# Four output stores of a two-stage attention kernel, moved behind a crossbar transfer in SyncE's order

## The chip, the core and the metric

The kernel runs on one core of one Trainium2 chip. Its metric is the device time of one execution in microseconds. Each engine of the core has its own instruction queue, which it works off in order: PE (TensorE) multiplies, DVE (VectorE) and ACT (ScalarE) read its results out of PSUM, POOL (GpSimd) masks and issues the loads, SP (SyncE) does no arithmetic here and issues DMAs. An engine waits for another one by semaphore. The DMA engines are shared by all queues.

## What is computed

Two stages, the second on the output of the first. Batch 8, 8 heads, 576 positions, head size 64; all inputs and the output are float32.

```python
def _attn_ref(q, k, v):                       # q, k, v: (8, 8, 576, 64)
    k_p = k.reshape(B, H, Sp, pool, D).mean(axis=3)      # 576 keys pooled by 8 to 72
    v_p = v.reshape(B, H, Sp, pool, D).mean(axis=3)
    scores = scale * np.matmul(q, k_p.transpose(0, 1, 3, 2))
    ...                                        # softmax over the 72 keys
    return np.matmul(attn, v_p)

def _moe_ref(x, w_gate, wq, wk, wv, wo):      # x: (8, 576, 512), 4 experts of size 64
    logits = x @ w_gate
    ...                                        # the two largest of four, softmax weights w
    for e in range(E):
        q = x @ wq[e]; k = x @ wk[e]; v = x @ wv[e]
        ...                                    # causal softmax attention over 576 positions
        ye = a @ v @ wo[e]
        ...                                    # out += weight of expert e * ye
    return out                                 # (8, 576, 512)
```

## The kernel before

The whole program is one list of tokens, the string SEQ (lines 622 to 693). The loop behind it (line 696) takes the tokens in order and lets each one emit its instructions; every engine's queue thus gets its instructions in the order in which they stand in SEQ. A token is a name with indices, a colon, the batch, and where needed the PSUM bank behind an @; a d at the end puts a copy on DVE instead of ACT, a p at the end of a y leaves the store to a later token. Capital letters are matmuls, small letters mostly what reads their result. The work of several batches is interleaved, so that batch 0 is in its last stage while batch 4 is in its first.

For this change these tokens matter:

- **L_q, L_k, L_v** (load, line 112): the loads of one batch's q in four quarters, and of k and v in three thirds each, issued by POOL (line 125). They change float32 into bfloat16 on the way. There are three raw buffers for each of q, k and v (NRAW, line 53), so the loads of a batch wait until the batch three earlier has been read.
- **u** (turn, line 292): a DVE transpose of one half of a batch's q (line 297). It needs all four quarters of that batch. u1:5 and u0:5 are those of batch 5.
- **T and t** (lines 559 and 564): PE transposes an expert pair's result, a copy brings it out of PSUM into oT. t02:1 is a copy of 64 columns of batch 1 on DVE; it stands in SEQ between u1:5 and u0:5, and it frees PSUM bank 2, into which O20:3 writes, the next output matmuls of the first stage that PE has in its order.
- **F** (crossbar, line 574): for batches 2 to 5 the same step is done by a DMA transpose issued by SP, from osc to oT; F01 and F11 carry the 64 positions behind 512 (line 577), F00 and F10 the first 512 (line 580).
- **Y and y** (lines 582 and 592): the output projection of 128 positions and its copy into an output tile ofin of 128 x 512 float32, 256 KB. The pool of these tiles has nine buffers (line 69), taken in turn; a new tile waits for the store of the tile nine earlier.
- **zs** (line 711, z in line 607): the store of such a tile, issued by SP (line 615; line 611 for the tile shared by two batches).

SP's whole work is two loads at the start, then the stores and the crossbar transfers. SP issues in the order of SEQ, and a transfer whose input isn't ready holds back all that stand behind it. In the order of before, after the two loads: zs3:0, zs1:0, zs2:0, zs3:1, F01:2, F00:2, F11:2, F10:2, F01:3, zs0:1, zs2:1, F00:3, zs3:2, F11:3, F10:3, zs1:1 and so on.

Y4:3 reads the tails that F01 and F11 of batches 2 and 3 bring; Y3:3, Y0:3, Y1:3 and Y2:3 read what F00:3 and F10:3 bring.

Of the kernel before, what the change touches and what calls it, by code (L numbers as in the profile page):

```python
# [21 lines left out]
def kernel(  # L22
# [584 lines left out]
    def z(b, c, queue):  # L607
# [42 lines left out]
        P_t0:2@7 v0:3d P_k1:3@5 L_q1:6 e11:4 t12:0d p_t0:2d g2:2 u1:5 V1:3@4 p_k1:3 L_q2:6 T02:1@2 E2:4@06 v1:3 D0:4@3  # L650
        t02:1d u0:5 e21:4 O20:3@2 PK:5@5 e20:4 D1:4@4 d0:4 o20:3 O11:4@0 kc:5 S02:2@6 d1:4 L_q3:6 S11:2@2 T12:1@1 kt:5d
        x1:4 P_q0:3@5 t12:1d g3:2 s11:2 L_v0:6 o11:4 B00:1@1 P_k0:3@4 bz00:1 s02:2 bg00:1 a11:2 b00:1 P_t0:3@0 p_q0:3d
        x0:4 S10:2@2 L_v1:6 p_t0:3d S12:2@6 O10:4@5 s10:2 p_k0:3d PV:5@0 a02:2 o10:4 O01:4@1 O00:4@4 vc:5 L_v2:6 D2:4@2
# [14 lines left out]
        x0:6 O01:6@4 a10:4 p_t0:5d e20:6 PV:7@5 b10:3 e21:6 O11:6@6 o01:6 O00:6@0 vc:7 F11:3 D2:6@7 O10:6@1 S01:4@2
        o00:6 d2:6 g0:4 S02:4@4 V3:5@7 o11:6 s01:4 F10:3 P_q1:5@0 v3:5d s02:4 a01:4 o10:6 S11:4@2 S01:5@6 p_q1:5d s11:4
        S00:4@4 a02:4 P_k0:6@1 g5:4 g1:5 g6:4 s01:5 g7:4 a11:4 Y4:3@0 g8:4 p_k0:6d V2:6@2 s00:4 a01:5 g9:4 Y1:1@3 v2:6d  # L670
        Y3:3@1 y4:3dp y1:1p a00:4 E0:7@46 y3:3p g2:5 zs1:1 Y0:0@3 zs4:3 g3:5 e01:7 g4:5 zs3:3 u1:7 V3:6@2 V1:6@1 y0:0p
        v3:6d Y2:2@0 g0:5 v1:6d e00:7 E1:7@26 zs0:0 y2:2dp Y4:1@1 e11:7 g5:5 zs2:2 B00:4@0 g6:5 y4:1dp P_k1:6@4 e10:7
        bz00:4 zs4:1 bg00:4 B11:4@1 b00:4 p_k1:6 g7:5 E2:7@26 x2:6 O01:7@0 bz11:4 g8:5 e21:7 D1:7@4 g9:5 O11:7@5 e20:7
        bg11:4 O20:6@6 d1:7 b11:4 O10:7@7 D2:7@2 O00:7@3 o20:6 F11:4 D0:7@1 x1:7 O20:7@4 P_q1:6@6 d0:7 o11:7 x0:7
        B10:4@1 o10:7 V0:6@5 d2:7 o01:7 x2:7 Y1:3@2 p_q1:6 P_q0:6@7 o20:7 v0:6 o00:7 y1:3p S02:5@4 bz10:4 p_q0:6 zs1:3
        S03:5@2 bg10:4 B01:4@6 b10:4 s03:5 g1:6 V0:7@7 s02:5 F10:4 a03:5 bz01:4 P_t0:6@2 bg01:4 b01:4 v0:7 S12:5@0
        a02:5 p_t0:6d g0:6 S11:5@4 F01:4 S00:6@6 s12:5 g2:6 V3:7@3 g3:6 g4:6 B01:5@2 s00:6 v3:7d F00:4 a12:5 Y2:3@0
        bz01:5 V4:7@3 bg01:5 s11:5 b01:5 V2:7@1 a00:6 y2:3dp Y0:3@2 v2:7 S10:5@6 a11:5 zs2:3 v4:7 y0:3dp S12:6@4
        S01:6@0 s10:5 B00:5@3 g5:6 zs0:3 g6:6 g7:6 P_t0:7@2 s12:6 g8:6 a10:5 g9:6 P_q0:7@6 p_t0:7d s01:6 bz00:5 a12:6
        bg00:5 Y1:2@2 b00:5 V1:7@7 p_q0:7d y1:2p F00:5 a01:6 S10:6@0 v1:7 S11:6@4 zs1:2 S02:6@2 s10:6 B10:5@6 g1:7  # L680
        F01:5 g2:7 Y0:2@7 s02:6 bz10:5 a10:6 B11:5@0 bg10:5 b10:5 P_k0:7@1 s11:6 bz11:5 a02:6 bg11:5 b11:5 F10:5
        B00:6@6 y0:2dp Y3:4@2 p_k0:7 a11:6 Y1:4@0 bz00:6 y3:4p zs0:2 bg00:6 F11:5 B11:6@1 b00:6 y1:4p S02:7@4 zs3:4
        bz11:6 S01:7@2 g0:7 bg11:6 S00:7@6 zs1:4 s02:7 b11:6 P_q1:7@0 g3:7 g4:7 g5:7 s00:7 g6:7 B10:6@1 a02:7 T00:6@4
        P_k1:7@5 bz10:6 bg10:6 p_q1:7 t00:6d a00:7 b10:6 s01:7 T11:6@4 Y1:5@6 p_k1:7d Y3:5@7 t11:6d y1:5p S03:6@0 a01:7
        S10:7@2 y3:5dp S11:7@4 s03:6 zs1:5 Y2:5@6 s10:7 g7:7 a03:6 zs3:5 g8:7 T10:6@7 Y0:5@0 t10:6d y2:5p B01:6@1 g9:7
        a10:7 y0:5dp B00:7@7 s11:7 Y0:4@2 zs2:5 bz01:6 zs0:5 B02:6@0 bg01:6 b01:6 y0:4p Y2:4@6 a11:7 bz02:6 bz00:7
        Y4:5@1 bg02:6 bg00:7 zs0:4 b02:6 y2:4p S12:7@2 b00:7 y4:5p S03:7@4 B10:7@0 zs2:4 T01:6@7 s12:7 Y1:6@6 bz10:7
        zs4:5 t01:6d B12:6@1 bg10:7 b10:7 Y3:6@7 y1:6p bz12:6 a12:7 T00:7@2 bg12:6 B01:7@0 b12:6 y3:6p zs1:6 t00:7d
        T10:7@6 Y2:6@1 bz01:7 t10:7 zs3:6 bg01:7 B11:7@7 b01:7 y2:6p Y1:7@6 bz11:7 s03:7 Y0:6@0 bg11:7 zs2:6 b11:7
        y1:7p Y0:7@1 a03:7 y0:6dp T11:7@7 zs1:7 T01:7@6 B02:7@4 t11:7d t01:7 T02:6@5 T12:6@2 zs0:6 B12:7@0 y0:7p bz02:7  # L690
        Y3:7@3 bg02:7 bz12:7 t02:6 t12:6 Y2:7@6 bg12:7 zs0:7 b12:7 y3:7p b02:7 T12:7@2 y2:7p T02:7@7 t12:7d zs3:7
        t02:7d zs2:7 Y4:7@0 ya4:7 yb4:7d
# [83 lines left out]
```

## Time and profile before

| what | us |
|---|---|
| median of three runs | 155.64 (155.61 to 155.65) |
| the profiled execution's own time | 155.6 |
| its span in the profile | 153.9 |
| PE busy | 143.7 (93%) |
| ACT busy | 137.5 (89%) |
| DVE busy | 125.2 (81%) |
| POOL busy | 88.9 (58%) |

The profile is of one execution. Its span begins with the first instruction on an engine and ends with the last; the execution's own time is 1.7 us longer. Times in the profile are microseconds from the span's start unless marked ns. L615 is line 615 of the kernel; a name like out_dram<-ofin says what is written from what. SPq is SP's instruction queue, PEld TensorE's weight load. A timeline gives the start, the duration, the engine, the line, the operation and its tiles, how many instructions are merged (x2), and in brackets how long the engine was idle before and what ended that. The table of stretches gives for each stretch its length, the busy time of PE, PEld, DVE, ACT and POOL with their counts of instructions, the clock granted to TensorE, the mean busy share of the DMA engines over the stretch in us and the GB/s moved. The chain of waits is the work that ended last, followed back from the end: at each step to what released it, or to the instruction ahead on the same engine.

### The profile page before, as it was taken

The numbers are of one execution on the slowest core, as the hardware profiler recorded it, in microseconds if no ns is written. First come the engines' busy times: TensorE is split into PE (matmuls) and PEld (weight loads), VectorE is DVE, ScalarE is ACT, GpSimd is POOL, SyncE is SP. The second block draws the span as 40 slices with busy tenths as digits, with TensorE's granted clock in tenths as the row PEclk, the third lists the DMA queues.
The fourth block names the chain that finished last, engine by engine and source line by source line (L and its number), as shares of the span: only waits on it lengthen the run. The fifth ranks groups of instructions, "written<-read, shape, count | busy, mean of one in ns | idle before, by whom it ended". The sixth has DMA issues, their size and how long they took to land.

```text
span 153.9 us, 5467 instructions
## 1 busy us (share of the span) xinstructions
PE 143.7 (93%) x2131; PEld 78.9 (51%) x2131; DVE 125.2 (81%) x407; ACT 137.5 (89%) x255; POOL 88.9 (58%) x160
## 2 busy tenths in 40 slices
PE   6698998999999999989999999999999999999970
PEld 2232453455654366445745565474556666546640
DVE  1863926889899889979999999999998987987860
ACT  3469579999999999989999999999999999999970
POOL 6996488999789988854999332053300344443200
PEclk9999999999999999999999999999999999999996
DMA  4999999999999999999999991361192343368894
GB/s 123 244 186 184 178 179 179 180 179 190 179 183 180 183 177 181 213 248 182 182 178 213 181 111 38 83 205 38 68 291 59 104 103 101 92 208 301 290 380 159
DMA packets 68746, 26.67 MB, mean 173 GB/s; under 512 B 62704, under 2 KB 63728, under 8 KB 68720
## 3 DMA queue, kind: packets, MB, share of 16 engines
q0 software_dynamic: 57264, 14.72, 95.9%
q1 hardware_dynamic: 11088, 10.88, 22.4%
q10 hardware_dynamic: 368, 0.72, 1.5%
q8 instruction: 16, 0.26, 0.7%
q14 instruction: 10, 0.08, 0.2%
HBM read 30.42 MB, written 9.44 MB: 259 GB/s over the span
## 4 chain that ended last, share of the span: by engine, by line
PE 65%; DMA 9%; ACT 9%; POOL 8%; issue 3%; DVE 3%; SPq 0%; DVEq 0%; POOLq 0%
PE psum L220 62%; DMA qraw<-in_q_dram 6%; ACT eta L330 4%; DMA xT<-in_k_dram 4%; POOL qraw L125 3%; POOL kraw L125 2%; ACT etb L493 2%; PE psum L208 2%; POOL etb L510 2%; PE psum L229 1%; DVE qT L297 1%; ACT rza L353 1%; ACT rza L349 1%; POOL vraw L125 1%; DVE kf L277 1%
## 5 line engine op out<-in xcount | busy, mean ns | idle before, releaser
L493 ACT ACTIVATE etb<-psum 128x1024 bf16<-128x1024 f32 x48 | 47.3, 1031 | 0.7 <-PE psum L220 0.4
L510 POOL TENSOR_SCALAR_AFFINE_SELECT etb<-etb 128x256 bf16<-128x256 bf16 x64 | 25.7, 414 | 30.0 <-ACT etb L493 29.4
L330 ACT ACTIVATE eta<-psum 96x1024 bf16<-96x1024 f32 (+1 forms) x48 | 36.1, 811 | 0.5 <-PE psum L220 0.2
L220 PEld LDWEIGHTS <-etb 128*128 128x128 bf16 x480 | 18.6, 97 | 7.6 <-issue 2.8
L376 DVE TENSOR_TENSOR xT<-psum,rza 128x512 bf16<-128x512 f32 x32 | 20.5, 682 | 2.0 <-ACT rza L353 1.9
L125 POOL DMA_DIRECT2D qraw<-in_q_dram x29 | 19.1, 660 | 4.4 <-DMA vraw<-in_v_dram 2.7
L220 PE MATMUL psum<-vaug,etb 128*128 128x65 bf16 x480 | 21.0, 193 | 0.0
L125 POOL DMA_DIRECT2D kraw<-in_k_dram x25 | 19.0, 766 | 3.3 <-PE psum L220 1.0
L125 POOL DMA_DIRECT2D vraw<-in_v_dram x24 | 18.5, 773 | 3.6 <-PE psum L220 1.6
L220 PE MATMUL psum<-wop,oT 128*128 128x512 bf16 (+1 forms) x74 | 20.3, 373 | 0.3 <-DVE oT L211 0.3
L220 PE MATMUL psum<-wvg,xT 128*128 128x260 bf16 x144 | 20.5, 274 | 0.0
L220 PE MATMUL psum<-xT,wqp 128*128 128x64 bf16 (+1 forms) x128 | 19.6, 286 | 0.0
L220 PE MATMUL psum<-xT,wkp 128*128 128x512 bf16 (+1 forms) x128 | 19.5, 286 | 0.0
L552 DVE TENSOR_TENSOR osc<-psum,gt 128x256 bf16<-128x256 f32 (+2 forms) x40 | 16.7, 423 | 1.0
L220 PE MATMUL psum<-qk 64*128 64x64 bf16 (+4 forms) x192 | 16.1, 277 | 0.2
L220 PEld LDWEIGHTS <-xT 128*128 128x128 bf16 x144 | 12.7, 97 | 6.3 <-issue 2.5
L211 DVE CAST qk<-psum 128x512 bf16<-128x512 f32 (+1 forms) x24 | 14.6, 616 | 1.1 <-PE psum L220 0.5
L297 DVE STREAM_TRANSPOSE qT<-qraw 128x576 f32<-128x576 f32 (+1 forms) x17 | 13.2, 790 | 2.8 <-DMA qraw<-in_q_dram 2.3
L220 PE MATMUL psum<-qT,kpT 32*128 32x64 bf16 (+1 forms) x256 | 13.3, 289 | 1.5 <-ACT eta L330 0.6
L211 ACT COPY ofin<-psum 128x512 f32<-128x512 f32 (+1 forms) x25 | 14.0, 584 | 0.8 <-PE psum L220 0.5
L220 PE MATMUL psum<-eta,vp 96*32 96x512 bf16 (+1 forms) x256 | 13.1, 288 | 0.9 <-DVE oT L211 0.7
L353 ACT ACTIVATE rza<-rza 128x512 f32<-128x512 f32 (+1 forms) x24 | 12.6, 527 | 0.4
(78 smaller groups left out, 215.9 us busy)
## 6 DMA issues: line engine op xcount, KB each, us to landing
out_dram<-ofin SPq DMA_DIRECT2D x32, 256.0 KB, 2.5
vraw<-in_v_dram POOLq DMA_DIRECT2D x24, 192.0 KB, 6.7
kraw<-in_k_dram POOLq DMA_DIRECT2D x21, 192.0 KB, 7.5
qraw<-in_q_dram POOLq DMA_DIRECT2D x28, 144.0 KB, 7.8
out_dram<-ofin SPq DMA_DIRECT2D x7, 128.0 KB, 2.5
xT<-in_q_dram ACTq DMA_DIRECT2D x2, 288.0 KB, 4.6
xT<-in_k_dram SPq DMA_DIRECT2D x2, 192.0 KB, 4.8
kraw<-in_k_dram POOLq DMA_DIRECT2D x4, 96.0 KB, 5.1
```

The lines of the kernel that those rows point to most:

```text
L125: nc.gpsimd.dma_start(out=dst, in_=src)
L208: nc.tensor.matmul(out=psum[rows, bank, :], lhsT=warm[:, rows], rhs=warm[:], start=True, stop=True)
L211: (nc.vector.tensor_copy if dve else nc.scalar.copy)(out=out, in_=in_)
L220: nc.tensor.matmul(out=out, lhsT=lhsT, rhs=rhs, start=start, stop=stop)
L229: nc.tensor.transpose(out=out[s], in_=in_[:, s], identity=ident[0:n, 0:n])
L297: nc.vector.transpose(out=dst.rearrange("p (a s n) -> p a n s", s=32, n=n)[:, :, own], in_=src.rearrange("p (a n d) -> p a n d", n=n, d=32 ...
L330: nc.scalar.activation(out=dst, in_=src, func=EXP, scale=ATT_EXP_SCALE)
L353: nc.scalar.activation(out=rz, in_=rz, func=EXP, scale=-1.0)
L376: nc.vector.tensor_tensor(out=xT[:, 2 * got[0][0] + t : 2 * got[-1][0] + t + 1 : 2, m + got[0][1].start : m + got[0][1].stop], in0=psum[:, ...
L493: nc.scalar.activation(out=et[:, ep, :, eo : eo + n], in_=psum[:, bank : bank + 2, 0:n], func=EXP, scale=MOE_EXP_SCALE,)
L510: nc.gpsimd.affine_select(out=blk, in_=blk, pattern=[[0, 2], [1, 128]], compare_op=ISGE, fill=0.0, base=0, channel_multiplier=-1,)
L552: nc.vector.tensor_tensor(out=osc(b, ep)[:, own, :].rearrange("p c (e d) -> p e c d", e=2), in0=o[:, :, :, 0:HD], in1=gt.to_broadcast([128 ...
```

## The change

Four tokens move in SEQ: zs3:0, zs1:0, zs2:0 (three tiles of batch 0) and zs3:1 (one of batch 1). They now stand together behind F01:3, the fifth crossbar transfer. All other tokens keep their order, and the remaining changed lines of the diff are the same tokens wrapped anew.

```diff
-        S00:2@2 y3:0p O01:3@6 o11:3 D2:3@1 PV:4@4 s00:2 L_v1:5 zs3:0 o01:3 O10:3@0 B01:1@7 vc:4d d2:3 kt:4 Y1:0@6
-        L_v2:5 bz01:1 v1:2 B02:1@1 o10:3 y1:0p a00:2 E0:4@24 bz02:1 bg01:1 x2:3 L_k0:6 bg02:1 b01:1 g0:2 zs1:0 Y2:0@6
-        b02:1 e00:4 u1:4 P_q1:3@7 L_k1:6 y2:0dp e01:4 E1:4@02 L_k2:6 p_q1:3d V0:3@6 zs2:0 e10:4 L_q0:6 g1:2 T12:0@4
+        S00:2@2 y3:0p O01:3@6 o11:3 D2:3@1 PV:4@4 s00:2 L_v1:5 o01:3 O10:3@0 B01:1@7 vc:4d d2:3 kt:4 Y1:0@6 L_v2:5
+        bz01:1 v1:2 B02:1@1 o10:3 y1:0p a00:2 E0:4@24 bz02:1 bg01:1 x2:3 L_k0:6 bg02:1 b01:1 g0:2 Y2:0@6 b02:1 e00:4
+        u1:4 P_q1:3@7 L_k1:6 y2:0dp e01:4 E1:4@02 L_k2:6 p_q1:3d V0:3@6 e10:4 L_q0:6 g1:2 T12:0@4 P_t0:2@7 v0:3d
...
-        a12:2 y3:1p g4:3 V1:4@2 g5:2 u0:6 L_q2:7 e01:5 zs3:1 P_k1:4@3 v1:4d L_q3:7 g0:3 g6:2 e00:5 E1:5@46 g5:3 a01:2
+        a12:2 y3:1p g4:3 V1:4@2 g5:2 u0:6 L_q2:7 e01:5 P_k1:4@3 v1:4d L_q3:7 g0:3 g6:2 e00:5 E1:5@46 g5:3 a01:2 g6:3
...
-        e01:6 p_q0:5d E1:6@24 bz00:3 F10:2 B11:3@0 bg00:3 b00:3 e10:6 V1:5@6 bz11:3 Y0:1@1 bg11:3 F01:3 e11:6 v1:5d
+        e01:6 p_q0:5d E1:6@24 bz00:3 F10:2 B11:3@0 bg00:3 b00:3 e10:6 V1:5@6 bz11:3 Y0:1@1 bg11:3 F01:3 zs3:0 zs1:0
+        zs2:0 zs3:1 e11:6 v1:5d B01:3@7 b11:3 Y2:1@6 y0:1p bz01:3 D0:6@0 bg01:3 b01:3 y2:1p PK:7@4 zs0:1 g1:4 O20:5@1
```

More of the change, by code (lines that the diff above doesn't have):

```diff
@@ L646 @@
         T00:0@4 d2:2 V1:2@5 L_q3:5 d1:3 o00:3 T02:0@2 V0:2@1 x2:2 a10:1 t00:0d t02:0 Y3:0@0 x1:3 o20:2 L_v0:5 v0:2d
-        S00:2@2 y3:0p O01:3@6 o11:3 D2:3@1 PV:4@4 s00:2 L_v1:5 zs3:0 o01:3 O10:3@0 B01:1@7 vc:4d d2:3 kt:4 Y1:0@6
-        L_v2:5 bz01:1 v1:2 B02:1@1 o10:3 y1:0p a00:2 E0:4@24 bz02:1 bg01:1 x2:3 L_k0:6 bg02:1 b01:1 g0:2 zs1:0 Y2:0@6
-        b02:1 e00:4 u1:4 P_q1:3@7 L_k1:6 y2:0dp e01:4 E1:4@02 L_k2:6 p_q1:3d V0:3@6 zs2:0 e10:4 L_q0:6 g1:2 T12:0@4
[L650 to L653, printed above, removed]
+        S00:2@2 y3:0p O01:3@6 o11:3 D2:3@1 PV:4@4 s00:2 L_v1:5 o01:3 O10:3@0 B01:1@7 vc:4d d2:3 kt:4 Y1:0@6 L_v2:5
+        bz01:1 v1:2 B02:1@1 o10:3 y1:0p a00:2 E0:4@24 bz02:1 bg01:1 x2:3 L_k0:6 bg02:1 b01:1 g0:2 Y2:0@6 b02:1 e00:4
+        u1:4 P_q1:3@7 L_k1:6 y2:0dp e01:4 E1:4@02 L_k2:6 p_q1:3d V0:3@6 e10:4 L_q0:6 g1:2 T12:0@4 P_t0:2@7 v0:3d
+        P_k1:3@5 L_q1:6 e11:4 t12:0d p_t0:2d g2:2 u1:5 V1:3@4 p_k1:3 L_q2:6 T02:1@2 E2:4@06 v1:3 D0:4@3 t02:1d u0:5
+        e21:4 O20:3@2 PK:5@5 e20:4 D1:4@4 d0:4 o20:3 O11:4@0 kc:5 S02:2@6 d1:4 L_q3:6 S11:2@2 T12:1@1 kt:5d x1:4
+        P_q0:3@5 t12:1d g3:2 s11:2 L_v0:6 o11:4 B00:1@1 P_k0:3@4 bz00:1 s02:2 bg00:1 a11:2 b00:1 P_t0:3@0 p_q0:3d x0:4
+        S10:2@2 L_v1:6 p_t0:3d S12:2@6 O10:4@5 s10:2 p_k0:3d PV:5@0 a02:2 o10:4 O01:4@1 O00:4@4 vc:5 L_v2:6 D2:4@2
         V2:3@3 o01:4 d2:4 s12:2 B10:1@0 a10:2 o00:4 V3:3@2 B11:1@1 bz10:1 L_k0:7 v2:3 bg10:1 E2:5@46 v3:3 b10:1 V4:3@3
@@ L656 @@
         g1:3 s01:3 T01:1@0 L_q0:7 T10:1@4 P_k0:4@5 t11:1d t10:1d t01:1d s01:2 g2:3 L_q1:7 Y3:1@4 g3:3 p_k0:4d E0:5@06
-        a12:2 y3:1p g4:3 V1:4@2 g5:2 u0:6 L_q2:7 e01:5 zs3:1 P_k1:4@3 v1:4d L_q3:7 g0:3 g6:2 e00:5 E1:5@46 g5:3 a01:2
-        g6:3 p_k1:4d V3:4@2 L_v0:7 e11:5 g7:2 T00:1@0 B00:2@3 g8:2 v3:4d a03:2 P_q0:4@1 e10:5 bz00:2 L_v1:7 t00:1d g9:2
+        a12:2 y3:1p g4:3 V1:4@2 g5:2 u0:6 L_q2:7 e01:5 P_k1:4@3 v1:4d L_q3:7 g0:3 g6:2 e00:5 E1:5@46 g5:3 a01:2 g6:3
+        p_k1:4d V3:4@2 L_v0:7 e11:5 g7:2 T00:1@0 B00:2@3 g8:2 v3:4d a03:2 P_q0:4@1 e10:5 bz00:2 L_v1:7 t00:1d g9:2
         bg00:2 B10:2@0 b00:2 a01:3 p_q0:4 S03:3@6 S11:3@4 L_v2:7 bz10:2 O20:4@2 s03:3 bg10:2 PV:6@1 b10:2 s11:3 a03:3
@@ L663 @@
         B11:2@1 s12:3 p_k0:5d F00:2 a00:3 E0:6@26 bz11:2 bg11:2 P_q0:5@0 x2:5 b11:2 a12:3 e00:6 u1:6 F11:2 B00:3@1
-        e01:6 p_q0:5d E1:6@24 bz00:3 F10:2 B11:3@0 bg00:3 b00:3 e10:6 V1:5@6 bz11:3 Y0:1@1 bg11:3 F01:3 e11:6 v1:5d
-        B01:3@7 b11:3 Y2:1@6 y0:1p bz01:3 D0:6@0 bg01:3 b01:3 y2:1p PK:7@4 zs0:1 g1:4 O20:5@1 d0:6 D1:6@7 zs2:1 kc:7
-        S12:4@2 F00:3 d1:6 P_k1:5@6 o20:5 s12:4 kt:7d g2:4 Y3:2@7 p_k1:5d x1:6 S03:4@0 S00:5@2 a12:4 S10:4@4 y3:2dp
-        s03:4 V2:5@6 s00:5 a03:4 g3:4 V4:5@0 zs3:2 g4:4 v2:5d B10:3@7 s10:4 v4:5d a00:5 P_t0:5@6 bz10:3 E2:6@02 bg10:3
@@ L668 @@
[L668 to L692, printed above, removed]
+        e01:6 p_q0:5d E1:6@24 bz00:3 F10:2 B11:3@0 bg00:3 b00:3 e10:6 V1:5@6 bz11:3 Y0:1@1 bg11:3 F01:3 zs3:0 zs1:0
@@ new lines @@
+        zs2:0 zs3:1 e11:6 v1:5d B01:3@7 b11:3 Y2:1@6 y0:1p bz01:3 D0:6@0 bg01:3 b01:3 y2:1p PK:7@4 zs0:1 g1:4 O20:5@1
+        d0:6 D1:6@7 zs2:1 kc:7 S12:4@2 F00:3 d1:6 P_k1:5@6 o20:5 s12:4 kt:7d g2:4 Y3:2@7 p_k1:5d x1:6 S03:4@0 S00:5@2
+        a12:4 S10:4@4 y3:2dp s03:4 V2:5@6 s00:5 a03:4 g3:4 V4:5@0 zs3:2 g4:4 v2:5d B10:3@7 s10:4 v4:5d a00:5 P_t0:5@6
+        bz10:3 E2:6@02 bg10:3 x0:6 O01:6@4 a10:4 p_t0:5d e20:6 PV:7@5 b10:3 e21:6 O11:6@6 o01:6 O00:6@0 vc:7 F11:3
+        D2:6@7 O10:6@1 S01:4@2 o00:6 d2:6 g0:4 S02:4@4 V3:5@7 o11:6 s01:4 F10:3 P_q1:5@0 v3:5d s02:4 a01:4 o10:6
@@ new lines @@
+        S11:4@2 S01:5@6 p_q1:5d s11:4 S00:4@4 a02:4 P_k0:6@1 g5:4 g1:5 g6:4 s01:5 g7:4 a11:4 Y4:3@0 g8:4 p_k0:6d V2:6@2
+        s00:4 a01:5 g9:4 Y1:1@3 v2:6d Y3:3@1 y4:3dp y1:1p a00:4 E0:7@46 y3:3p g2:5 zs1:1 Y0:0@3 zs4:3 g3:5 e01:7 g4:5
+        zs3:3 u1:7 V3:6@2 V1:6@1 y0:0p v3:6d Y2:2@0 g0:5 v1:6d e00:7 E1:7@26 zs0:0 y2:2dp Y4:1@1 e11:7 g5:5 zs2:2
+        B00:4@0 g6:5 y4:1dp P_k1:6@4 e10:7 bz00:4 zs4:1 bg00:4 B11:4@1 b00:4 p_k1:6 g7:5 E2:7@26 x2:6 O01:7@0 bz11:4
+        g8:5 e21:7 D1:7@4 g9:5 O11:7@5 e20:7 bg11:4 O20:6@6 d1:7 b11:4 O10:7@7 D2:7@2 O00:7@3 o20:6 F11:4 D0:7@1 x1:7
@@ new lines @@
+        O20:7@4 P_q1:6@6 d0:7 o11:7 x0:7 B10:4@1 o10:7 V0:6@5 d2:7 o01:7 x2:7 Y1:3@2 p_q1:6 P_q0:6@7 o20:7 v0:6 o00:7
+        y1:3p S02:5@4 bz10:4 p_q0:6 zs1:3 S03:5@2 bg10:4 B01:4@6 b10:4 s03:5 g1:6 V0:7@7 s02:5 F10:4 a03:5 bz01:4
+        P_t0:6@2 bg01:4 b01:4 v0:7 S12:5@0 a02:5 p_t0:6d g0:6 S11:5@4 F01:4 S00:6@6 s12:5 g2:6 V3:7@3 g3:6 g4:6 B01:5@2
+        s00:6 v3:7d F00:4 a12:5 Y2:3@0 bz01:5 V4:7@3 bg01:5 s11:5 b01:5 V2:7@1 a00:6 y2:3dp Y0:3@2 v2:7 S10:5@6 a11:5
+        zs2:3 v4:7 y0:3dp S12:6@4 S01:6@0 s10:5 B00:5@3 g5:6 zs0:3 g6:6 g7:6 P_t0:7@2 s12:6 g8:6 a10:5 g9:6 P_q0:7@6
@@ new lines @@
+        p_t0:7d s01:6 bz00:5 a12:6 bg00:5 Y1:2@2 b00:5 V1:7@7 p_q0:7d y1:2p F00:5 a01:6 S10:6@0 v1:7 S11:6@4 zs1:2
+        S02:6@2 s10:6 B10:5@6 g1:7 F01:5 g2:7 Y0:2@7 s02:6 bz10:5 a10:6 B11:5@0 bg10:5 b10:5 P_k0:7@1 s11:6 bz11:5
+        a02:6 bg11:5 b11:5 F10:5 B00:6@6 y0:2dp Y3:4@2 p_k0:7 a11:6 Y1:4@0 bz00:6 y3:4p zs0:2 bg00:6 F11:5 B11:6@1
+        b00:6 y1:4p S02:7@4 zs3:4 bz11:6 S01:7@2 g0:7 bg11:6 S00:7@6 zs1:4 s02:7 b11:6 P_q1:7@0 g3:7 g4:7 g5:7 s00:7
+        g6:7 B10:6@1 a02:7 T00:6@4 P_k1:7@5 bz10:6 bg10:6 p_q1:7 t00:6d a00:7 b10:6 s01:7 T11:6@4 Y1:5@6 p_k1:7d Y3:5@7
@@ new lines @@
+        t11:6d y1:5p S03:6@0 a01:7 S10:7@2 y3:5dp S11:7@4 s03:6 zs1:5 Y2:5@6 s10:7 g7:7 a03:6 zs3:5 g8:7 T10:6@7 Y0:5@0
+        t10:6d y2:5p B01:6@1 g9:7 a10:7 y0:5dp B00:7@7 s11:7 Y0:4@2 zs2:5 bz01:6 zs0:5 B02:6@0 bg01:6 b01:6 y0:4p
+        Y2:4@6 a11:7 bz02:6 bz00:7 Y4:5@1 bg02:6 bg00:7 zs0:4 b02:6 y2:4p S12:7@2 b00:7 y4:5p S03:7@4 B10:7@0 zs2:4
+        T01:6@7 s12:7 Y1:6@6 bz10:7 zs4:5 t01:6d B12:6@1 bg10:7 b10:7 Y3:6@7 y1:6p bz12:6 a12:7 T00:7@2 bg12:6 B01:7@0
+        b12:6 y3:6p zs1:6 t00:7d T10:7@6 Y2:6@1 bz01:7 t10:7 zs3:6 bg01:7 B11:7@7 b01:7 y2:6p Y1:7@6 bz11:7 s03:7
@@ L693 @@
+        Y0:6@0 bg11:7 zs2:6 b11:7 y1:7p Y0:7@1 a03:7 y0:6dp T11:7@7 zs1:7 T01:7@6 B02:7@4 t11:7d t01:7 T02:6@5 T12:6@2
+        zs0:6 B12:7@0 y0:7p bz02:7 Y3:7@3 bg02:7 bz12:7 t02:6 t12:6 Y2:7@6 bg12:7 zs0:7 b12:7 y3:7p b02:7 T12:7@2 y2:7p
+        T02:7@7 t12:7d zs3:7 t02:7d zs2:7 Y4:7@0 ya4:7 yb4:7d
     """
```

## The prediction

> **What bounds the kernel now.** I read the page first, then the chain of waits, then the timelines of PE, DVE, ACT and SP around the one break in that chain, and last the stretches of half a microsecond for the DMA rate.
>
> ```profile
> span 153.9 us, 5467 instructions
> PE 143.7 (93%) x2131; PEld 78.9 (51%) x2131; DVE 125.2 (81%) x407; ACT 137.5 (89%) x255; POOL 88.9 (58%) x160
> DMA  4999999999999999999999991361192343368894
> out_dram<-ofin SPq DMA_DIRECT2D x32, 256.0 KB, 2.5
> ```
>
> TensorE (PE) is the fullest engine. The row of DMA tenths says that the DMA engines are full up to slice 23 of 40 (about 92 us: all loads of q, k and v lie there) and mostly free afterwards. Now the chain of waits, in order of time, from its last DMA on:
>
> ```profile
> 58.38 8.66 DMA qraw<-in_q_dram
> ...
> 67.16 0.78 DVE qT L297
> 67.94 0.09 DVE oT L211
> ...
> 82.39 53.34 PE psum L220 x846
> ```
>
> The fourth quarter of batch 5's q (token L_q3:5) is issued at 58.38 and lands 8.66 us later; the DVE transpose u1:5 waits for it, the small copy t02:1 stands behind it in DVE's order, and PE waits for that copy because it frees the PSUM bank of O20:3. From there on, 68.06, the chain is PE alone, nearly to the end of the span; the last row is its longest piece. So what comes before 68.06 can be shortened only through this landing, and what comes after it only by less PE work or by keeping PE from waiting. How large is the break? The timelines of DVE, PE and ACT there (start, duration, engine, operation, and in brackets the idle time before it with its releaser):
>
> ```profile
> 65.89 0.16 DVE L419 TENSOR_TENSOR s<-lo 128x4 f32<-128x4 f32 x1
> 67.16 0.78 DVE L297 STREAM_TRANSPOSE qT<-qraw 128x576 f32<-128x576 f32 x1 [1.11 <-DMA qraw<-in_q_dram]
> 67.86 0.15 DVE L211 COPY oT<-psum 128x64 bf16<-128x64 bf16 x1
> 66.59 0.22 PE L229 MATMUL psum<-ident,osc 128*128 128x128 bf16 x1
> 66.97 0.40 PE L220 MATMUL psum<-eta,onesd 96*32 96x512 bf16 x4
> 68.06 0.30 PE L220 MATMUL psum<-eta,vp 96*32 96x64 bf16 x16 [0.69 <-DVE oT L211]
> 68.96 0.60 ACT L349 ACTIVATE rza<-psum 128x512 f32<-128x512 f32 x1 [0.66 <-PE psum L220]
> ```
>
> DVE idles 1.11 us, PE 0.69 us, ACT 0.66 us, all for that one landing. That is the prize that can be had here: 0.69 us of PE.
>
> **The change part by part.** No instruction is added or removed: four stores of 256 KB leave their places on SP. Where they stand now (SP's timeline: all four, then the second and the third alone), how long the first takes to land, and the DMA rate (the last two numbers of a stretch are the DMA share and GB/s):
>
> ```profile
> 59.83 20.35 SPq L615 DMA_DIRECT2D out_dram<-ofin  x4
> DMA to landing us min/median/max: 5.8/5.8/5.8
> 62.15 0.36 SPq L615 DMA_DIRECT2D out_dram<-ofin  x1
> 64.20 0.33 SPq L615 DMA_DIRECT2D out_dram<-ofin  x1
> 63.00:63.50 0.50, 0.50 (x4) 0.17 (x2) 0.50 (x1) 0.50 (x2) 0.03 (x1) 1.00 1.83 180
> 63.50:64.00 0.50, 0.50 (x10) 0.12 (x8) 0.50 (x2) 0.50 (x1) 0.50 (x1) 1.00 1.64 247
> 64.00:64.50 0.50, 0.50 (x10) 0.21 (x3) 0.50 (x2) 0.45 (x2) 0.50 (x2) 1.00 1.25 325
> 64.50:65.00 0.50, 0.50 (x12) 0.46 (x11) 0.47 (x4) 0.50 (x1) 0.50 (x2) 1.00 1.48 225
> 66.00:66.50 0.50, 0.50 (x6) 0.34 (x5) 0.05 (x1) 0.47 (x2) 0.00 (x0) 1.00 1.63 258
> 66.50:67.00 0.50, 0.50 (x24) 0.29 (x22) 0.00 (x0) 0.50 (x2) 0.47 (x1) 1.00 1.19 326
> ```
>
> *Taken away: the stores out of the load stream.* Loads alone run at 180 GB/s, steadily, which is a queue that the DMA engines and not GpSimd set. The first store (zs3:0, issued at 59.83, landed 5.8 us later, at 65.6) is the bump from 63.5 to 65.0: 0.5 x (247 + 325 + 225) = 398 KB moved, where loads alone would have moved 1.5 x 180 = 270 KB. The store is 262 KB, so the loads got 136 KB instead of 270, a loss of 134 KB, at 180 KB per us 0.74 us. The second (zs1:0, issued at 62.15) is the bump that begins at 66.0 and is not over when the load lands at 67.03. Its surplus over 180 GB/s up to then is 0.5 x (78 + 146) = 112 KB; in the first bump 128 KB of surplus went with 134 KB of loads lost, so I take as much as the surplus here, 112 KB or 0.62 us. The third was issued at 64.20, 2.8 us ahead of that landing; the first two needed 3.7 and 3.9 us until their bytes moved, so I count it at nothing here. Sum: the load lands 0.74 + 0.62 = 1.36 us earlier, at about 65.67. Bounds: 0.74 if only the first store counts, 2.1 if all three do.
>
> *What that does.* DVE is done with the instruction ahead at 65.89 + 0.16 = 66.05, so u1:5 starts there instead of at 67.16. It ends at 66.83; the copy's input (the transpose by PE at 66.59, 0.22 long) is ready at 66.81; the copy ends at about 67.0. PE is busy until 66.97 + 0.40 = 67.37. So PE goes on at 67.37 instead of 68.06: **minus 0.69 us**. Even the low bound does it: 0.74 us earlier puts the copy's end at 67.27. ACT, which waited 0.66 us for PE's next result, is free at 68.96 - 0.66 = 68.30, about where that result then is. DVE has 1.11 - 0.69 = 0.42 us more than it needs. Three engines move together, which is why I carry 0.69 to the end. Past that point the chain shows no further DMA, so the 0.7 us each that the third and the fourth store (the fourth ends its issue at 59.83 + 20.35 = 80.18) take from loads were hidden behind PE and are worth nothing.
>
> *Added: four issues behind F01:3.* SP's timeline there, the DVE result that the fifth row waits for, PE's first uses of what the crossbar brings, and the landing times of all sixteen crossbar transfers:
>
> ```profile
> 96.33 2.15 SPq L577 DMA_TRANSPOSE oT<-osc  x1
> 98.58 1.00 SPq L615 DMA_DIRECT2D out_dram<-ofin  x2
> 99.67 1.25 SPq L580 DMA_TRANSPOSE oT<-osc  x1
> 101.02 0.53 SPq L615 DMA_DIRECT2D out_dram<-ofin  x1
> 103.57 1.52 SPq L577 DMA_TRANSPOSE oT<-osc  x1
> 105.15 1.27 SPq L580 DMA_TRANSPOSE oT<-osc  x1
> 103.00 0.55 DVE L552 TENSOR_TENSOR osc<-psum,gt 128x384 bf16<-128x384 f32 x1
> 107.86 0.59 PE L220 MATMUL psum<-wop,oT 128*128 128x512 bf16 x2
> 108.75 1.02 PE L220 MATMUL psum<-wop,oT 128*128 128x512 bf16 x4
> DMA to landing us min/median/max: 2.3/2.6/4.2
> ```
>
> F01:3 is the row at 96.33. Queued behind the four on SP are zs0:1 and zs2:1 (98.58), F00:3 (99.67), zs3:2 (101.02), F11:3 (103.57) and F10:3 (105.15). Two stores take from 98.58 to 99.67, 0.55 us each, so four hold SP for 2.2 us. SP now idles from 101.02 + 0.53 = 101.55 to 103.57, 2.0 us, because F11:3 waits for DVE's result at 103.55. So F00:3 comes 2.2 us late and F11:3 and F10:3 0.2 us late. With the median landing of 2.6 us F10:3 lands at 107.75; its first reader is Y3:3, the second pair of the row at 108.75, about 109.2: 1.45 us of room. F11:3 lands at 103.57 + 2.6 = 106.2 for Y4:3 at 107.86: 1.7 us of room. F00:3 lands near 104.5 for the same 109.2. The whole stretch moves 0.69 us earlier together. So this part costs **nothing**, with this cover: 2.0 us of idle SP and 1.45 us before Y3:3. If a store held SP for more than (2.0 + 1.45) / 4 = 0.86 us, PE would pay. Bounds of one store's cost from other rows:
>
> ```profile
> 136.40 6.50 SPq L615 DMA_DIRECT2D out_dram<-ofin  x8
> 146.00:148.00 2.00, 2.00 (x32) 1.37 (x30) 1.65 (x7) 1.54 (x6) 0.29 (x1) 1.00 1.00 377
> ```
>
> At least the 0.33 of the row at 64.20; at most 6.50 / 8 = 0.81 where SP issues without pause. Full DMA moves 377 GB/s, thus 0.70 us for a store. All lie under 0.86; I take 0.55, the rows of that very place.
>
> *Output buffers.* The pool has 9 ofin buffers. In the order of the y tokens the tenth is y3:3, which takes over the buffer of y3:0, and it stands behind PE's matmuls at 108.75. The stores would have landed by about 103. No wait.
>
> Sum: 155.6 (profiled execution: 153.9 of span and 1.7 around it) - 0.69 + 0 = 154.9; the runs' median is 155.64, so 154.95.
>
> *A rule that speaks against it.* The row is the 0.69 us of PE above, behind a load that shared its time with stores for which nobody was waiting. The Trainium skill (DMA: Bandwidth & Descriptors, section Rules for kernel authors) advises to issue a DMA early, compute, and wait on its semaphore late, so that its fixed cost overlaps; by that the early stores cost nothing where they stand and the change is worth nothing, 155.64, as in the first rival below. The bumps of the trace say that on full DMA engines an early store is paid by the loads, and the rule does not speak of that.
>
> **The rivals.**
>
> *The stores were hidden anyway*, or the wait comes back under another name: PE finds its next bank, or ACT its next input, no earlier. For it: DVE, PE and ACT are all nearly full from 60 to 68 us, so there are many such couplings. Against it: each of the three shows its idle time in the rows above, and all three end with the same landing. Time: 155.64.
>
> *The crossbar comes too late.* Slower, through one place: F10:3 lands behind a row of stores in the same DMA queue. Its price: the slowest of the sixteen crossbar transfers took 4.2 us to land, 1.6 over the median. With four stores at 0.70 us of full DMA, 2.8 us, less the 2.0 us of idle SP, F10:3 would be 1.6 + 0.8 = 2.4 us late. The room of 1.45 us decides: from there on PE waits, here 0.95 us, and from 1.45 + 0.69 = 2.14 us of lateness on the kernel is slower than before. Time: 155.64 - 0.69 + 0.95 = 155.9. Against it: SP's own rows need only 0.2 us, and the DMA is mostly free at that time.
>
> *DVE gives more.* If DVE and not PE sets the pace after 68 us (it is nearly as full), its whole 1.11 us comes through: 154.53. Against it: the chain names PE alone.
>
> *The change does not do what it says*: a buffer or a completion count that ties other work to the stores' places. Nothing of the order of the y tokens supports it. Time: 155.6.
>
> **How the numbers follow.** Forecast 0.62 (154.95); hidden anyway 0.14; crossbar late 0.14; DVE's larger gain 0.06; not as said 0.04. A measurement of this kernel can tell about 0.2% (0.31 us) from no change. Faster: 0.62 + 0.06 = 0.68; within: 0.14 + 0.04 = 0.18; slower: 0.14. The range goes from 154.5 (DVE's whole idle time) over no change up to 155.8, and leaves out the upper part of the crossbar case.
>
> **What would show it.** SP has no store between 59 and 90 us, and the DMA rate stays at 180 GB/s without the bumps. The q load of batch 5 takes about 7.3 us instead of 8.66 to land. DVE's transpose follows its predecessor without idle time, and PE has no 0.69 us of idle time near 67 us. Four more stores stand behind F01:3, F00:3 is issued near 101.2 (2.2 us late on a timeline that is 0.69 us ahead), F11:3 near 103.0, and PE shows no wait before the output matmuls near 107 to 109 us. I am wrong if PE still breaks at 67 us with another releaser, if the break has moved to a later load, or if the output projections of batch 3 wait for a crossbar transfer.

## The result and the profile after

The changed kernel takes 155.35 us (median of ten runs, 154.72 to 155.50) beside 155.78 us of the kernel before, run along with it; the ratio is 0.9962 with a 95% interval of 0.9946 to 0.9977. On the 155.64 us of before that is 0.59 us less, with an interval of 0.36 to 0.84; the two medians themselves differ by 0.43 us. The forecast was 154.95, its range 154.5 to 155.8.

The profiled execution of the changed kernel took 155.49 us. The page's head and its row of DMA tenths:

```profile
span 153.8 us, 5466 instructions
DMA  4999999999999999999999902399192433457994
```

Counted from 0, the slices are full up to number 22 instead of 23 (a slice is 3.8 us), and slices 26 and 27 (100 to 108 us) are newly full: there the stores go out, and the crossbar transfers behind them. The stretches around 60 to 68 us, then the landing of the fourth quarter of batch 5's q:

```profile
60.00:62.00 2.00, 2.00 (x40) 1.13 (x39) 2.00 (x6) 2.00 (x6) 1.64 (x3) 1.00 1.82 185
64.00:66.00 2.00, 2.00 (x31) 1.07 (x30) 1.90 (x6) 1.97 (x3) 1.84 (x4) 1.00 1.82 179
66.00:68.00 2.00, 2.00 (x44) 1.25 (x44) 1.89 (x9) 1.99 (x6) 1.71 (x3) 1.00 1.82 180
DMA to landing us min/median/max: 7.0/7.0/7.0
```

The number ahead of the GB/s is the packets' time as a share of the 16 engines' time. It is a ratio and not in us, and it goes above 1 where packets overlap: 1.82 for loads at 180 GB/s. The bumps are gone, the rate is about 180 GB/s in every stretch, and the load, issued at 59.07, lands 7.0 us later where it took 8.66. The timelines of DVE and PE at the old break, and at a new one near 48 us; the last row is DVE at that place in the kernel before, without a wait:

```profile
66.64 0.16 DVE L419 TENSOR_TENSOR s<-lo 128x4 f32<-128x4 f32 x1
66.71 0.77 DVE L297 STREAM_TRANSPOSE qT<-qraw 128x576 f32<-128x576 f32 x1
67.95 0.29 PE L220 MATMUL psum<-eta,vp 96*32 96x64 bf16 x16
47.15 1.44 DVE L297 STREAM_TRANSPOSE qT<-qraw 128x576 f32<-128x576 f32 x2 [1.38 <-DMA qraw<-in_q_dram]
49.67 0.27 PE L229 MATMUL psum<-ident,osc 128*128 128x128 bf16 x2 [0.60 <-DVE qk L211]
45.84 1.44 DVE L297 STREAM_TRANSPOSE qT<-qraw 128x576 f32<-128x576 f32 x2
```

DVE's transpose u1:5 follows its predecessor at once and PE has no idle time before 67.95. But PE goes on only 0.11 us sooner than before (68.06), because this execution came to the place late: batch 4's q landed late, its transpose waited 1.38 us at 47.15, PE stood for 0.60 us. None of the four stores is issued before 59.8 us, in either kernel. So the profile of the changed kernel alone cannot say where the gain is; the table below can. It gives, for every profile taken, the shift against the first profile of before: the difference of the start times of the same ACT instructions, as the median over those within 2.5 us of the given time.

| kernel, its profiled time | 46 | 60 | 70 | 80 | 90 | 100 | 111 | 148 us |
|---|---|---|---|---|---|---|---|---|
| changed, 155.49 | -0.04 | +0.79 | -0.01 | -0.11 | -0.13 | -0.13 | -0.13 | -0.12 |
| changed again (e1), 155.19 | -0.06 | +0.49 | -0.32 | -0.41 | -0.43 | -0.43 | -0.43 | -0.43 |
| before again (e12), 155.59 | +0.01 | +0.28 | -0.43 | -0.43 | -0.10 | -0.09 | -0.09 | -0.10 |
| one store (e2), 155.37 | +0.60 | +0.69 | -0.11 | -0.21 | -0.23 | -0.23 | -0.23 | -0.23 |
| last store (e3), 155.69 | -0.05 | +0.15 | -0.42 | -0.42 | +0.05 | +0.05 | +0.05 | +0.05 |
| weights late (e4), 154.75 | -0.11 | -0.06 | -0.77 | -0.87 | -0.89 | -0.89 | -0.89 | -0.89 |
| weights late, stores early (e5), 155.29 | +0.15 | +0.24 | -0.33 | -0.32 | -0.27 | -0.34 | -0.33 | -0.34 |
| behind first (e6), 155.79 | -0.13 | -0.13 | -0.81 | -0.90 | -0.93 | +0.03 | +0.03 | +0.02 |
| behind seventh (e7), 156.41 | -0.05 | +0.81 | 0.00 | -0.10 | -0.12 | -0.12 | +0.78 | +0.77 |
| weights late, behind first (e8), 155.40 | +0.21 | +0.28 | -0.43 | -0.53 | -0.55 | -0.19 | -0.18 | -0.19 |
| behind eighth (e9), 155.51 | +0.54 | +0.62 | -0.18 | -0.28 | -0.30 | -0.30 | -0.30 | -0.09 |
| weights late, behind eighth (e10), 155.53 | +0.03 | +0.30 | -0.51 | -0.60 | -0.62 | -0.62 | -0.62 | -0.39 |
| weights late again (e11), 155.18 | +0.32 | +0.31 | -0.36 | -0.45 | -0.48 | -0.48 | -0.48 | -0.48 |

In both profiles of the changed kernel 0.90 us is gained between 60 and 80 us, and what the execution had lost ahead of 60 us (0.79 and 0.49) is subtracted from it. The late part, SP's timeline behind F01:3, the landings of F00:3 and of F11:3 and F10:3, a stretch of the DMA, PE at Y4:3, and what its weight load waited for (us in total, times, longest):

```profile
95.94 1.15 SPq L577 DMA_TRANSPOSE oT<-osc  x1
97.19 4.27 SPq L615 DMA_DIRECT2D out_dram<-ofin  x6
101.55 1.39 SPq L580 DMA_TRANSPOSE oT<-osc  x1
103.65 1.11 SPq L577 DMA_TRANSPOSE oT<-osc  x1
104.81 1.69 SPq L580 DMA_TRANSPOSE oT<-osc  x1
DMA to landing us min/median/max: 5.6/5.6/5.6
DMA to landing us min/median/max: 3.4/3.8/4.2
100.00:102.00 2.00, 2.00 (x37) 1.46 (x34) 1.97 (x8) 2.00 (x5) 1.41 (x4) 1.00 1.01 380
107.74 0.59 PE L220 MATMUL psum<-wop,oT 128*128 128x512 bf16 x2
PEld L220 <- DMA oT<-osc: 0.2, 1, 0.2
```

The issues come where the sum put them (F00:3 at 101.55, F11:3 at 103.65), but the landings do not. The six stores in a row run at 380 GB/s, and the crossbar transfers, in the same queue, land behind them: F00:3 at 107.15, F11:3 at 103.65 + 4.2 = 107.85, just when Y4:3 wants it (107.74). The wait of 0.2 us for it is TensorE's weight load, and no shift between 100 and 111 us comes of it. The room was used up to the last tenth.

### The profile page after: what moved, and what is told of

Read it like the earlier page. It is cut to its first block, busy times and chain, and to the rows that moved or that the text cites. A ratio compares the mean times of both kernels' runs of the same rounds, so it can differ in the third digit from the quotient of the medians.

```text
span 153.8 us, 5466 instructions
## 1 busy us (share of the span) xinstructions
PE 143.7 (93%) x2131; PEld 79.5 (52%) x2131; DVE 124.4 (81%) x407; ACT 137.5 (89%) x255; POOL 89.0 (58%) x160
## 4 chain that ended last, share of the span: by engine, by line
PE 64%; DMA 16%; POOL 13%; issue 2%; DVE 2%; POOLq 0%; DVEq 0%
PE psum L220 63%; DMA qraw<-in_q_dram 10%; DMA wst_k<-in_moe_wk_dram 6%; POOL kraw L125 4%; POOL vraw L125 3%; POOL qraw L125 3%; PE psum L229 2%; POOL etb L510 1%; POOL wst_v L160 1%; POOL wst_q L160 1%; DVE qT L297 1%; POOL wst_g L160 0%; DVE osc L552 0%; DVE ofin L211 0%; DVE oT L211 0%
## 5 line engine op out<-in xcount | busy, mean ns | idle before, releaser
L220 PE MATMUL psum<-qT,kpT 32*128 32x64 bf16 (+1 forms) x256 | 12.8, 289 | 1.6 <-ACT eta L330 0.7
L208 PE MATMUL psum<-warm 128*128 128x512 bf16 x41 | 12.0, 437 | 1.3 <-DVE onesd L176 1.3
```

The costliest lines, as they stand in the source:

```text
L208: nc.tensor.matmul(out=psum[rows, bank, :], lhsT=warm[:, rows], rhs=warm[:], start=True, stop=True)
L220: nc.tensor.matmul(out=out, lhsT=lhsT, rhs=rhs, start=start, stop=stop)
```

## The experiments

There were twelve runs, each timed in five rounds beside the kernel before.

**e1, the changed kernel again.**

> The changed kernel once more, for a second profile. Theory (loads pace both kernels, at another place): in its first profile the landing of batch 4's q at 47.0 us came 1.3 us later than in the profile of before and took back 0.8 us; that is chance of the load queue and not the change. Here a time between 154.7 and 155.5 us, and the break near 48 us differs from 0.60 us of PE idle time in proportion to the time. Rival (the change itself causes that delay): the landing is again near 47.0 and PE again 0.7 us late at 60 us.

Measured: 155.22 us (154.83 to 155.96), ratio 0.9962 (0.9943 to 0.9980), the same ratio as the first time. Its timelines near 48 us:

```profile
46.85 1.44 DVE L297 STREAM_TRANSPOSE qT<-qraw 128x576 f32<-128x576 f32 x2 [1.11 <-DMA qraw<-in_q_dram]
49.37 0.27 PE L229 MATMUL psum<-ident,osc 128*128 128x128 bf16 x2 [0.33 <-DVE qk L211]
```

A smaller break there (PE 0.33 us instead of 0.60) goes with a profiled time 0.30 us shorter, as the theory had it. That the delay is not the change's own is seen better in e6, which has the same instructions up to 90 us and no delay at 60 us, and in e12, the kernel before, with 0.28 us of it. The break near 48 us is not its only source: in e2 and e9 DVE does not wait there, and the executions were already 0.60 and 0.54 us late at 46 us.

**e2, one store only.** Its diff, and that of e3:

```diff
-L_v1:5 zs3:0 o01:3
+L_v1:5 o01:3
...
-F01:3 e11:6
+F01:3 zs3:0 e11:6
```

```diff
-e01:5 zs3:1 P_k1:4@3
+e01:5 P_k1:4@3
...
-F01:3 e11:6
+F01:3 zs3:1 e11:6
```

> Only the first store (zs3:0) goes behind F01:3, the other three stay. Theory: one store out of the load stream brings the q load of batch 5 0.74 us earlier, which is enough for the 0.69 us of PE; same time as the whole change, 155.0 to 155.4, no idle PE near 67 us. Rival (the whole 1.4 us of both stores is needed, or the stores are not the cause): PE still idles 0.3 to 0.7 us near 67 us and the time is 155.5 to 155.7.

Measured: 155.37 us (155.06 to 155.77), ratio 0.9963 (0.9949 to 0.9976): the ratio of the whole change with a quarter of it. DVE near 67 us, and the landing of the fourth quarter of batch 5's q, issued at 58.98:

```profile
66.62 0.77 DVE L297 STREAM_TRANSPOSE qT<-qraw 128x576 f32<-128x576 f32 x1
DMA to landing us min/median/max: 7.0/7.0/7.0
```

There is no idle time, and the load lands as soon after its issue as with all four stores gone. One store of 262 KB is enough.

**e3, the last store only.**

> Only the fourth store (zs3:1, issued at 79.9 us before) goes behind F01:3, the first three stay. Theory: it stands after the break, so it is worth nothing: 155.6 to 155.8, PE idle 0.7 us near 67 us as before. Rival (the gain comes from freer DMA after 68 us): 155.2 to 155.4.

Measured: 155.69 us (155.45 to 156.22), ratio 0.9995 (0.9984 to 1.0007): worth nothing, as forecast. The profile shows something else than expected, though. DVE, then PE:

```profile
66.74 0.78 DVE L297 STREAM_TRANSPOSE qT<-qraw 128x576 f32<-128x576 f32 x1 [0.58 <-DMA qraw<-in_q_dram]
67.64 0.30 PE L220 MATMUL psum<-eta,vp 96*32 96x64 bf16 x16 [0.16 <-DVE oT L211]
82.34 0.48 PE L220 MATMUL psum<-vaug,etb 128*128 128x65 bf16 x10 [0.32 <-POOL etb L510]
```

The break at 67 us is only 0.16 us of PE, and PE is 0.42 us ahead at 80 us. Then a second break at 82 us, where PE waits for a mask of POOL, takes it all back. The second gate is the subject of e12.

**e4, the output weights' load later.** In addition to the change, one load of 256 KB goes from ahead of the break near 48 us to behind it.

```diff
-d1:1 W4:0 o01:1
+d1:1 o01:1
...
-L_q3:4 S00:1@4
+L_q3:4 W4:0 S00:1@4
```

> The changed kernel, and the load of the output weights (256 KB, token W4:0, issued near 32 us) goes behind L_q3:4, the last quarter of batch 4's q. Theory (after the change the landing of batch 4's q at 46 to 47 us is what paces the rest, and its spread is the spread of the times): that landing comes 1.4 us earlier, DVE and PE do not wait for it, and the time is 154.5 to 154.8 in all executions. Rival (nothing paces after the break is gone but the engines, and the spread has another cause): 154.7 to 155.5 as the changed kernel.

Measured: 154.81 us (154.60 to 155.19), ratio 0.9936 (0.9920 to 0.9952). Batch 4's and batch 5's transposes on DVE:

```profile
45.62 1.42 DVE L297 STREAM_TRANSPOSE qT<-qraw 128x576 f32<-128x576 f32 x2
66.10 0.78 DVE L297 STREAM_TRANSPOSE qT<-qraw 128x576 f32<-128x576 f32 x1
```

Neither waits. In the table, the five profiles with the late load fall back by at most 0.27 us between 46 and 60 us, the others by up to 0.86. So the load that was put ahead of the break for nothing (its first reader is the output projection near 59 us) costs time that it need not, though not in every execution, and it is not all that is lost ahead of 60 us: e11 was 0.32 us late at 46 us already. The ratio rests on six executions here and on six in e11. The profiled execution is 0.89 us ahead of before at the end, where the two of the changed kernel were 0.12 and 0.43 ahead. e11 repeats it.

**e5, the same without the change.** The load moved as in e4, the four stores where they were before.

> The kernel before with only the load of the output weights moved behind L_q3:4, the four stores where they were. Theory (before, the landing of batch 5's q at 67 us sets the time, and it is set by all bytes ahead of it, of which none leaves here): PE comes earlier or equal to 67 us and idles there 0.7 to 1.0 us; time 155.6 to 155.8, as before. Rival (the two load savings add independently of each other): 155.2 to 155.4.

Measured: 155.58 us (155.19 to 156.33), ratio 0.9990 (0.9972 to 1.0007). No gain that can be told, as forecast. Whether the load helps less here than with the stores gone (0.0010 of the ratio against 0.0026) is not shown; the intervals are wider than the difference. In the profiled execution (155.29) DVE waited 0.41 us at 66.83 and PE not at all, less than the 0.7 to 1.0 us expected.

**e6, the four stores behind the first crossbar transfer.** They leave their old places as in the change; the diff, like those of e7 and e9, shows only where they go.

```diff
-F01:2 s00:3 u0:7
+F01:2 zs3:0 zs1:0 zs2:0 zs3:1 s00:3 u0:7
```

> The four stores behind the first crossbar transfer (F01:2, near 91 us) instead of the fifth. Theory (the late position costs PE nothing, and the time is set before 68 us): same as the changed kernel, 154.8 to 155.5, ratio 0.995 to 0.998; F00:3, F11:3 and F10:3 land about 2.6 us after their issue again instead of 5.6, 4.2 and 3.4. Rival (the late stores cost some PE time through the crossbar): up to 0.3 us faster than the changed kernel.

Measured: 155.82 us (155.44 to 156.22), ratio 1.0001 (0.9986 to 1.0017). Both theory and rival missed: the gain is gone. SP's timeline, the landing of F10:2, and PE:

```profile
91.12 2.04 SPq L615 DMA_DIRECT2D out_dram<-ofin  x4
95.88 2.51 SPq L580 DMA_TRANSPOSE oT<-osc  x1
DMA to landing us min/median/max: 3.8/3.8/3.8
99.70 0.39 PE L220 MATMUL psum<-wop,oT 128*128 128x512 bf16 x1 [0.78 <-DMA oT<-osc]
```

PE is 0.92 us ahead until 97 us, stands at Y3:2 for F10:2, which lands at 95.88 + 3.8 = 99.68, and is 0.03 us behind afterwards. That is the rival of the prediction in which the crossbar comes too late, at another transfer: batch 2's F10:2 has less room than batch 3's. In the kernel before it was the slowest of the sixteen to land (94.97 + 4.2 = 99.2), and Y3:2 began at 99.47. F00:3, F11:3 and F10:3 landed after 2.6, 3.1 and 2.5 us, close to what was expected.

**e7, behind the seventh.**

```diff
-F11:3 D2:6@7
+F11:3 zs3:0 zs1:0 zs2:0 zs3:1 D2:6@7
```

> The four stores behind the seventh crossbar transfer (F11:3), so that only F10:3 stands behind them. This uses up the cover on purpose. Theory (crossbar transfers queue behind stores on SP and in the DMA, and the room at the fifth place was some tenths of a microsecond): F10:3 is issued 2.2 us late and lands 4 to 6 us after its issue, at 110.5 to 112 us, where PE wants it near 109: PE idles 1.5 to 3 us there, and the time is 156.5 to 158. Rival (stores and crossbar transfers do not hold each other up enough to matter): as the changed kernel, 154.8 to 155.5.

Measured: 156.22 us (155.90 to 157.31), ratio 1.0029 (1.0008 to 1.0050): slower than before. SP, the landing of F10:3, PE:

```profile
104.96 2.03 SPq L615 DMA_DIRECT2D out_dram<-ofin  x4
107.04 1.37 SPq L580 DMA_TRANSPOSE oT<-osc  x1
DMA to landing us min/median/max: 3.1/3.1/3.1
110.17 0.39 PE L220 MATMUL psum<-wop,oT 128*128 128x512 bf16 x1 [0.73 <-DMA oT<-osc]
```

The mechanism is as expected, its size smaller: F10:3 landed at 110.14, and the shift grew by 0.90 us (from -0.12 to +0.78) and not by 1.5 to 3.

**e8, e4 with the stores behind the first transfer.**

> Both: the output weights' load behind L_q3:4, and the four stores behind the first crossbar transfer. Theory: as the run with the late output weights, 154.6 to 154.9, since the late position cost nothing there either. Rival (it did cost): 154.3 to 154.5.

Measured: 155.56 us (155.03 to 155.87), ratio 0.9985 (0.9969 to 1.0000). Missed for the same reason as e6: the table shows the step from -0.55 to -0.19 between 90 and 100 us, and at Y3:2 PE again waits for a crossbar transfer (0.19 us).

**e9 and e10, behind the eighth transfer,** without and with the later load of the weights.

```diff
-F10:3 P_q1:5@0
+F10:3 zs3:0 zs1:0 zs2:0 zs3:1 P_q1:5@0
```

> The four stores behind the eighth crossbar transfer (F10:3, near 104.5 us): the next crossbar transfer comes only near 116 us, so nothing of the crossbar stands right behind them. The tiles they free are wanted from 109.5 us on (y3:3); the stores would be issued near 106.5 and land from 109 us on. Theory (at the fifth place the stores fit just into the room and cost PE 0 to 0.3 us): 154.8 to 155.5, equal to the changed kernel or 0.2 us faster; F00:3, F11:3 and F10:3 land in 2.6 us. Rival (the nine output tiles are too few for that delay): ACT or DVE wait for a store near 110 us, 155.6 or more.

> The output weights' load behind L_q3:4 and the four stores behind the eighth crossbar transfer. Theory: 154.6 to 154.9, as with the stores at the fifth place (the place has no price where nothing waits). Rival (the late landings of the crossbar at the fifth place cost there too): 154.3 to 154.5.

Measured: e9 155.44 us (155.14 to 155.81), ratio 0.9962 (0.9947 to 0.9978), equal to the change, without a wait for an output tile near 110 us; F00:3, F11:3 and F10:3 landed after 2.7, 2.6 and 2.5 us, as expected. e10 155.25 us (155.01 to 155.53), ratio 0.9961 (0.9945 to 0.9977), 0.3 us more than e11, the same kernel as e4, in the same series. In both profiles, and in no other, the shift worsens by 0.2 us between 111 and 148 us; DVE in e10 has this wait, which the changed kernel does not have:

```profile
135.81 0.29 DVE L211 COPY oT<-psum 128x256 bf16<-128x256 bf16 x1 [0.28 <-ACT etb L493]
```

The releaser that is named there is not a plausible one for this copy, and what it does wait for was not found. So the eighth place seems to have a price of its own far behind it, of unknown cause.

**e11 and e12, e4 and the kernel before once more.**

> The run with the late output weights and the stores at the fifth place once more, beside the one before on the same chip: 154.6 to 155.2 as the first time.

> The kernel before once more, for a second profile and for the spread between equal kernels: ratio 0.999 to 1.001. Theory (the landing of batch 5's q sets its time, and chance in the load queue ahead of it is hidden): PE's shift at 60 us against the first profile may be anything from 0 to 0.8 us, but PE goes on within 0.2 us of 68.06 and the time is 155.5 to 155.9. Rival (chance in the load queue comes through here as in the changed kernel): a shift at 60 us is still there at 70 us.

Measured: e11 154.98 us (154.64 to 155.28), ratio 0.9937 (0.9915 to 0.9958), as the first time. e12 155.79 us (155.46 to 156.49), ratio 0.9999 (0.9984 to 1.0014). The timelines of e12, DVE, PE and POOL:

```profile
66.73 0.78 DVE L297 STREAM_TRANSPOSE qT<-qraw 128x576 f32<-128x576 f32 x1 [0.42 <-DMA qraw<-in_q_dram]
82.20 0.48 PE L220 MATMUL psum<-vaug,etb 128*128 128x65 bf16 x10 [0.18 <-POOL etb L510]
80.41 1.31 POOL L125 DMA_DIRECT2D qraw<-in_q_dram  x2
81.73 0.42 POOL L510 TENSOR_SCALAR_AFFINE_SELECT etb<-etb 128x256 bf16<-128x256 bf16 x1
```

Here the expectation of one gate at 68 us failed: PE was 0.43 us ahead at 70 us. But neither does that lead come through. At 82 us PE waits for a mask that stands on POOL behind load issues. The lead shrinks to 0.10 us, as in e3 from 0.42 to nothing. So the kernel before has two gates, both set by the load queue: batch 5's q at 67 us, and POOL at 82 us. In its first profile POOL's load issues at 68.75 and 70.59 us waited 0.77 and 1.18 us for earlier loads to land; in the changed kernel the same two, at 67.46 and 68.53, waited 0.29 and 0.41. The mask in the first profile of before, in e2 and in the changed kernel:

```profile
81.82 0.42 POOL L510 TENSOR_SCALAR_AFFINE_SELECT etb<-etb 128x256 bf16<-128x256 bf16 x1
81.20 0.42 POOL L510 TENSOR_SCALAR_AFFINE_SELECT etb<-etb 128x256 bf16<-128x256 bf16 x1
80.47 0.42 POOL L510 TENSOR_SCALAR_AFFINE_SELECT etb<-etb 128x256 bf16<-128x256 bf16 x1
```

It is done at 82.24, 81.62 and 80.89 us. The stores that leave the load stream thus relieve both gates, and in e2 one store is enough for both.

## Why the prediction was right, point by point

**What bounds the kernel.** Right in the main: loads held PE, and taking a store away ahead of them gave the gain (e2). Incomplete: the prediction said that behind 68.06 nothing but PE's own work counts. The second gate at 82 us was not visible in the first profile, since PE came to it just in time there.

**The load lands 1.36 us earlier.** Right in kind, too large in size. The packets of the loads (q0) and of SP's queue (q1) in the kernel before, from 63.5 to 65.0 us, with their MB:

```profile
q0 software_dynamic: 564, 0.14, 94.3%
q1 hardware_dynamic: 141, 0.26, 51.3%
```

The loads moved 0.14 MB where they would have moved 0.27, which bears out the 0.74 us of the first store. But the load landed at 59.07 + 7.0 = 66.1 us instead of 67.0, 1.0 us earlier, and in e2, with only the first store gone, at 58.98 + 7.0 = 66.0. The second store's 0.62 us should not have been added: its bytes began to move at 66.0, about when the load lands once the first store is gone. The 8.66 us to landing were also the longest seen. The other profiles with the first store in place have 7.8 (e12), 8.0 (e3) and 8.1 us (e5) and land at 66.6 to 66.7. Against those the load is about 0.7 us earlier, the price of one store.

**PE gains 0.69 us, carried to the end.** Right in kind; that the number fits is partly luck. The profile from which it was read shows the largest break of four: with the first store in place PE stood there for 0.69 us (before), 0.16 us (e3) and not at all (e5, e12). In e3 and e12 the mask at 82 us took back most or all of what PE had gained. In both profiles of the changed kernel PE gains 0.90 us between 60 and 80 us; the 0.2 us over 0.69 were not traced to a wait. From these 0.90 goes what an execution has lost ahead of 60 us, 0.79 and 0.49 here. The prediction had neither of the two. Before, such a loss is absorbed by the gates at 67 and 82 us: the second profile of before is 0.28 us late at 60 us and 0.10 us early at the end. In the changed kernel it comes through in full, and its profiled times differ as the losses do. The measured 0.59 us (0.36 to 0.84) cannot be told from 0.69.

**The third and fourth store are worth nothing.** Shown for the fourth (e3, ratio 0.9995). The second and the third were not tried alone, but e2, in which they stay, has the ratio of the whole change.

**Four issues behind F01:3 cost nothing.** True in its result (no shift between 90 and 111 us), wrong in its working. The term that was mis-sized is the landing: F11:3 and F10:3 were given 2.6 us and took 4.2 and 3.4, F00:3 5.6. I costed a store at 0.55 us of SP and put the 0.70 us of DMA into a bound, and of the DMA queue I counted four stores, though the two that already stood there join them. The 1.7 us of room before Y4:3 were down to nothing. e6 and e7, one place with less room and one with less distance, lose 0.95 and 0.90 us, more than the whole gain of the runs.

**The rivals.** Hidden anyway: refuted by e2 (0.9963) against e3 (0.9995). The crossbar too late: it did not happen at the fifth place and did at the first and seventh, with PE idle for 0.78 and 0.73 us where 0.95 had been priced. DVE gives more (154.53): the best single run of the changed kernel was 154.72, so an execution that lost little ahead of 60 us does come near it; whether DVE is the reason was not shown. The change not doing what it says: refuted by the timeline of SP.

**The rule against it.** The four stores cost the loads their time where they stood, though nobody waited for them. The Trainium skill (DMA: Bandwidth & Descriptors, section Rules for kernel authors) has DMAs issued early and waited for late, so that the fixed setup cost overlaps with compute; by that alone the change would have been worth nothing, and the ratio of 0.9962 says otherwise. What the early stores cost here is not setup but bytes on DMA engines that loads already filled.

**A faster kernel than both.** The change together with the later load of the output weights: 0.9936 and 0.9937 of before in two series (e4, e11).

## What to carry to other kernels

In this kernel, with the DMA engines full of loads, a store that nobody waited for was not free: the load behind it paid for it, 0.7 us for 262 KB. The question is whether that load, or another behind it, is one that an engine waits for. Putting a store off is right only into a place whose followers in the same queue have room for the store's time on the DMA engines, counted with all stores beside it and not by its issue. One profile shows only the gate that binds in that execution: take a second one of the same kernel before carrying a break's length to the end. And when a break goes, look for the next one behind and ahead of it: here the gain was cut by what the gates had been hiding, and one load moved out of the way gave another 0.4 us with the stores at the fifth place.
